# Attention and two MLPs on one core: seven block products in place of eight for x times w_in, and the MLP work put in order by a list scheduler

## The chip, the core and the metric

One core of a Trainium2 chip. The time is device microseconds of one execution. Engines: PE is TensorE (matrix products; PEld is its weight load), DVE is VectorE, ACT is ScalarE, POOL is GpSimd, SP issues the transfers. SBUF is the working memory, PSUM the eight banks (128 rows of 512 fp32) into which PE writes.

## The reference

Attention with rotary embedding over q, k, v (2 batches, 8 heads, 576 positions, 64 wide), then two MLPs one after the other on the 1152 tokens of width 512. The MLPs are what the change touches:

```python
def _moe_ref(x, w_in, w_out):           # x 1152x512, w_in 512x2048, w_out 2048x512
    h = x @ w_in
    sp = np.where(h > 20.0, h, np.log1p(np.exp(np.minimum(h, 20.0))))
    g = h * np.tanh(sp)
    return (g @ w_out).astype(np.float32)

def _moe2_ref(x, w_in, w_out):
    h = x @ w_in
    g = h * (1.0 / (1.0 + np.exp(-1.702 * h)))
    return (g @ w_out).astype(np.float32)
```

## The kernel before, in words

**Precision.** Each fp32 operand of an MLP product is kept as two tiles, a high part (the value rounded to fp32r by an ACT copy) and a low part (value minus high, by DVE). A product is the sum of three: high-high, high-low, low-high (`TERMS`, `X_LAST`). So every 128-deep step of a matrix product costs three matmuls.

**Weights.** w_in and w_out lie in HBM as float64. `Weights` (L474) fetches one piece of 128x512 numbers (512 KB) with one DMA from SP (L490), narrows it to fp32 bits with three DVE operations (L517, L520, L523), and splits it: ACT makes the high part (L504), DVE the low part (L505). `W.step` does the next of these five operations whenever the MLP code calls it, so the order of DVE and ACT is that of the calls.

**MLP one.** The 2048 columns of h are done in two halves of eight blocks of 128 (`FC` = 8). `phase_in` (L605) takes from `units_in` one unit after the other, a 128x384 piece of h transposed (block j of d_ff, third u of the tokens), 12 matmuls of 128x128 by 384 columns each (`mm_in`, L574). ACT applies the activation out of PSUM (L620) and copies the high part into g (L621), DVE subtracts the low part (L611). `phase_out1` (L627) then multiplies g by w_out (L641, 384 columns), keeps the first half's sums in `acc` (ACT, L1114) and adds the second half's (DVE, L1119), and splits the result into x2, the second MLP's input (L1120, L1121).

**MLP two** is the same with `phase_out2` (L652): here g is the stationary operand and w_out moves, 512 columns a matmul (L655). ACT keeps the first half (L1134), DVE adds the second (L1137), SP stores each tile of 128 tokens (L1148).

**Order.** Attention and the first ten steps of MLP one are ordered by `Plan`, a planner with costs and due times. After `plan.run()` every engine follows the order in which the MLP code is written. In PSUM, `mbank` hands out eight banks in turn.

Of the kernel before, what the change touches and what calls it, by code (L numbers as in the profile page):

```python
# [22 lines left out]
def kernel(  # L23
# [12 lines left out]
    nc = tc.nc  # L36
# [13 lines left out]
    FC = KF // 2  # L50
# [404 lines left out]
    def in_piece(w, j):  # L455
        return w[:, 128 * j:128 * j + 128].rearrange("(k p) c -> p k c", p=128)

    ORDER = ((0, 0), (1, 0), (2, 0), (0, 1), (1, 1), (2, 1), (3, 0), (3, 1))

    pieces = []  # L460
    for c in range(2):
        pieces += [in_piece(w_in1, FC * c + j) for j in range(FC)]
        for d, f in ORDER:
            f0 = 128 * FC * c + 512 * f
            pieces.append(w_out1[f0:f0 + 512, 128 * d:128 * d + 128].rearrange("(k p) c -> p k c", p=128))
    for c in range(2):
        pieces += [in_piece(w_in2, FC * c + j) for j in range(FC)]
        for f in range(FC):
            f0 = 128 * (FC * c + f)
            pieces.append(w_out2[f0:f0 + 128, :])  # L470

    RING = 11

    class Weights:  # L474
# [4 lines left out]
        def __init__(self):  # L479
            self.late = None  # L480
            self.loaded = self.narrowed = self.split = self.freed = 0
            self.raw, self.flat, self.parts = {}, {}, {}
            self.todo = deque()
            self.eng, self.ahead = DVE, 0

        def load_one(self):
            n = self.loaded
            t = self.raw[n] = wp.tile([128, 512], w_in1.dtype, tag="wraw", name="wraw", bufs=2)
            src = pieces[n]
            SP.dma_start(out=t.rearrange("p (k c) -> p k c", k=4) if len(src.shape) == 3 else t, in_=src)  # L490
            self.loaded += 1

        def load(self):
            while self.loaded < len(pieces) and self.loaded - self.narrowed < self.ahead:
                self.load_one()

        def start(self):
            if self.split < self.narrowed and self.split - self.freed < (RING if self.late else 3):
                n = self.split
                pool, bufs = (wp, 3) if n % RING < 3 else (self.late, RING - 3)  # L500
                r = self.flat.pop(n)
                t = self.parts[n] = pool.tile([128, 2, 512], F32R, tag="whl", name="whl", bufs=bufs)
                self.todo.extend([
                    lambda: ACT.activation(out=t[:, 0], in_=r, func=AF.Copy),  # L504
                    lambda: self.eng.tensor_tensor(out=t[:, 1], in0=r, in1=f32(t[:, 0]), op=ALU.subtract),  # L505
                ])
                self.split += 1
            elif self.narrowed < self.loaded and self.narrowed - self.split < 2:
                n = self.narrowed
                raw = self.raw.pop(n)  # L510
                if WIDE:
                    words = raw.bitcast(I32).rearrange("p (n w) -> p n w", w=2)
                    lo, hi = words[:, :, 0], words[:, :, 1]
                    t = wp.tile([128, 512], I32, tag="wf", name="wf", bufs=2)
                    self.flat[n] = f32(t)
                    self.todo.extend([
                        lambda: DVE.tensor_scalar(  # L517
                            t, hi, 3, 0x3FFFFFF8, op0=ALU.logical_shift_left, op1=ALU.bitwise_and
                        ),
                        lambda: DVE.scalar_tensor_tensor(  # L520
                            out=t, in0=hi, scalar=-0x40000000, in1=t, op0=ALU.bitwise_and, op1=ALU.bitwise_or
                        ),
                        lambda: DVE.scalar_tensor_tensor(  # L523
                            out=t, in0=lo, scalar=29, in1=t, op0=ALU.logical_shift_right, op1=ALU.bitwise_or
                        ),
                    ])
                else:
                    self.flat[n] = raw
                self.narrowed += 1

        def step(self, count=1):
            for _ in range(count):
                if not self.todo:
                    self.load()
                    self.start()
                if not self.todo:
                    return
                self.todo.popleft()()
            if not self.todo:
                self.load()  # L540

        def get(self, n):
            while self.split <= n or self.todo and n == self.split - 1:
                self.step()
            return self.parts[n]

        def free(self, n):

            del self.parts[n]
            while self.freed < self.split and self.freed not in self.parts:  # L550
                self.freed += 1
# [8 lines left out]
    def mbank(name):  # L560
        nbank[0] = nbank[0] % 8 + 1
        if nbank[0] <= 6:
            return pools["b"].tile([128, 512], F32, tag="b", name=name)
        return pvps if nbank[0] == 7 else bank(name)
# [14 lines left out]
    def units_in(n0, src, full=0):  # L579


        early = {}
        for j, u in sorted(((j, u) for j in range(2) for u in range(3)), key=lambda x: x[1] if full else 0):
            early[j, u] = mbank("h")
            mm_in(early[j, u], W.get(n0 + j), src, u, range(KD if u < full else KD - 1))
            yield None
        late = X_LAST[2:] if full else X_LAST
        for j, u in early:
            if u >= full > 0:
                mm_in(early[j, u], W.get(n0 + j), src, u, (KD - 1,), X_LAST[:2])  # L590
                yield None
        for j in range(FC):
            for u in range(3):
                if j < 2:
                    ps = early.pop((j, u))
                    if u >= full:
                        mm_in(ps, W.get(n0 + j), src, u, (KD - 1,), late)
                else:
                    ps = mbank("h")
                    mm_in(ps, W.get(n0 + j), src, u, range(KD))  # L600
                if u == 2:
                    W.free(n0 + j)
                yield j, u, ps[:, 0:UN]

    def phase_in(units, g, func):  # L605

        late = deque()

        def low():
            gl, t, gh = late.popleft()  # L610
            DVE.tensor_tensor(out=gl, in0=t, in1=f32(gh), op=ALU.subtract)  # L611

        for unit in units:
            W.step(2)
            if unit is None:
                continue
            j, u, ps = unit
            t = pools["tp"].tile([128, UN], F32, tag="t", name="t")
            gh, gl = (g[:, i, j, cols(u)] for i in range(2))
            ACT.activation(out=t, in_=ps, func=func)  # L620
            ACT.activation(out=gh, in_=t, func=AF.Copy)  # L621
            late.append((gl, t, gh))
            if len(late) > 1:
                low()
        low()

    def phase_out1(n0, g, evac):  # L627


        acc = {}  # L630
        steps = [(i, u) for i in range(len(ORDER)) for u in range(3)]
        steps.insert(11, steps.pop(8))
        for i, u in steps:
            d, half = ORDER[i]
            w = W.get(n0 + i)
            if half == 0:
                acc[d, u] = mbank("acc")
            ps = acc[d, u]
            for f in range(4):
                for wl, gl in TERMS:  # L640
                    PE.matmul(  # L641
                        out=ps[:, 0:UN], lhsT=w[:, wl, 128 * f:128 * f + 128], rhs=g[:, gl, 4 * half + f, cols(u)],
                        start=(half == 0 and f == 0 and (wl, gl) == TERMS[0]),
                        stop=(half == 1 and f == 3 and (wl, gl) == TERMS[2]),
                    )
            if u == 2:
                W.free(n0 + i)
            if half == 1:
                evac(d, u, ps[:, 0:UN])
            W.step(2)  # L650

    def phase_out2(n0, g, evac, by_tile):  # L652
        def mm(ps, t, f, w):
            for gl, wl in TERMS:
                PE.matmul(  # L655
                    out=ps, lhsT=g[:, gl, f, 128 * t:128 * t + 128], rhs=w[:, wl, :],
                    start=(f == 0 and (gl, wl) == TERMS[0]), stop=(f == FC - 1 and (gl, wl) == TERMS[2]),
                )
        ps = {t: mbank("acc") for t in range(5)}
# [536 lines left out]
```

## Time and profile before

| | |
|---|---|
| median of 3 runs | 557.73 us (557.49 to 558.0) |
| the profiled execution | 556.88 us; its trace spans 555.0 us |
| PE busy | 544.6 us, 98% of the span |
| DVE, ACT, POOL busy | 341.0, 257.5, 90.1 us |
| chain that ended last | 90% PE, 6% DVE, 2% DMA |
| granted TensorE clock | full (2.4 GHz) in every slice up to the last |

The MLPs begin at 147 us (first matmul of L574) and fill the rest. An engine's busy time is the union of its instructions. A matmul's record is longer than the time until the next one can start, since matmuls overlap in the array; what a stream of them costs is read from where the first and the last start, not from the mean of one.

### The profile page before, as it was taken

What the parts mean: (1) busy time and instruction counts of PE and PEld (TensorE: products, weight loads), DVE (VectorE), ACT (ScalarE), POOL (GpSimd) and SP (SyncE); (2) the same over time, 40 slices, a digit from 0 to 9 for tenths busy, and PEclk for the clock granted to TensorE, in tenths of its full rate; (3) what the DMA queues carried; (4) which work ended last, traced back from release to release, by engine and by line L of the source; (5) the groups of instructions that cost most, each with busy time, mean ns of one, the idle gap of its engine ahead of it and who ended that gap; (6) DMA issues with size and microseconds to landing.
All of it is one profiled execution on the core that took longest, in us unless ns stands there. A gap on an engine that the chain in (4) does not pass through costs nothing.

```text
span 555.0 us, 8983 instructions
## 1 busy us (share of the span) xinstructions
PE 544.6 (98%) x3517; PEld 489.9 (88%) x3517; DVE 341.0 (61%) x684; ACT 257.5 (46%) x544; POOL 90.1 (16%) x86
## 2 busy tenths in 40 slices
PE   8999999999999999999999999999999999999996
PEld 7876777777879999999999999999988899998885
DVE  6889889989629874356976458676520537820020
ACT  2887778887418741223865122275512126741000
POOL 3777868544100000000000000000000000000000
PEclk9999999999999999999999999999999999999999
DMA  7856596675505434233342322422310123200032
GB/s 201 186 121 162 112 211 151 133 118 137 145 1 152 124 107 150 64 123 118 119 139 85 114 77 76 141 83 81 96 57 1 61 88 121 73 1 0 1 113 57
DMA packets 82537, 56.90 MB, mean 103 GB/s; under 512 B 47224, under 2 KB 78272, under 8 KB 82496
## 3 DMA queue, kind: packets, MB, share of 16 engines
q1 hardware_dynamic: 81504, 56.12, 38.4%
q8 instruction: 27, 0.44, 0.3%
q10 hardware_dynamic: 992, 0.23, 0.2%
q14 instruction: 14, 0.11, 0.1%
HBM read 43.45 MB, written 2.40 MB: 83 GB/s over the span
## 4 chain that ended last, share of the span: by engine, by line
PE 90%; DVE 6%; DMA 2%; ACT 1%; issue 1%; SPq 1%; DVEq 0%; ACTq 0%
PE h L574 32%; PE acc L641 16%; PE acc L655 16%; PE st L261 5%; PE pvps L574 4%; PE pvps L421 4%; PE pvps L641 2%; PE st L334 2%; DVE spill L274 2%; PE pvps L655 2%; PE tps L232 2%; PE pvps L429 2%; DMA raw_v<-in_v_dram 1%; DVE pt L304 1%; DMA rest<-in_q_dram 1%
## 5 line engine op out<-in xcount | busy, mean ns | idle before, releaser
L574 PE MATMUL h<-x,whl 128*128 128x384 f32 x1008 | 179.5, 335 | 0.0
L574 PEld LDWEIGHTS h<-x,whl 128*128 128x128 f32 x1008 | 174.8, 188 | 2.9 <-issue 2.5
L505 DVE TENSOR_TENSOR whl<-wf,whl 128x512 fp32r<-128x512 f32 x62 | 42.9, 692 | 94.9 <-ACT whl L504 94.9
L655 PE MATMUL acc<-whl,g 128*128 128x512 f32 x384 | 88.9, 389 | 0.0
L641 PE MATMUL acc<-g,whl 128*128 128x384 f32 x504 | 88.6, 334 | 0.0
L641 PEld LDWEIGHTS acc<-g,whl 128*128 128x128 f32 x504 | 87.5, 188 | 0.0
L655 PEld LDWEIGHTS acc<-whl,g 128*128 128x128 f32 x384 | 72.0, 188 | 14.9
L611 DVE TENSOR_TENSOR g<-t,g 128x384 fp32r<-128x384 f32 x96 | 53.1, 554 | 27.1 <-ACT g L621 27.1
L504 ACT ACTIVATE whl<-wf 128x512 fp32r<-128x512 f32 x64 | 40.2, 628 | 62.1 <-DVE wf L523 42.8
L274 DVE CUSTOM_DVE_ANT_1 spill<-st,shift 128x576 f16<-128x576 f32 x72 | 54.4, 755 | 8.6 <-PE st L261 3.5
L620 ACT ACTIVATE t<-h 128x384 f32<-128x384 f32 x84 | 40.5, 482 | 35.8 <-PE h L574 35.8
L621 ACT ACTIVATE g<-t 128x384 fp32r<-128x384 f32 x96 | 50.6, 527 | 3.1
L289 ACT ACTIVATE e<-st,nm 128x576 f32<-128x576 f32 x64 | 47.1, 739 | 4.8 <-DVE nm L274 4.0
L261 PE MATMUL st<-qk 64*128 64x288 f32 (+1 forms) x432 | 44.3, 311 | 1.6 <-ACT e L289 1.5
L520 DVE SCALAR_TENSOR_TENSOR wf<-wraw,wf 128x512 int32<-128x512 int32 x64 | 44.2, 691 | 1.6
L261 PEld LDWEIGHTS st<-qk 64*128 64x128 f32 (+1 forms) x432 | 34.1, 185 | 12.6 <-ACT e L289 6.6
L523 DVE SCALAR_TENSOR_TENSOR wf<-wraw,wf 128x512 int32<-128x512 int32 x64 | 44.1, 689 | 1.4
L308 POOL TENSOR_TENSOR p<-e,p 128x576 f16<-128x576 f32 x28 | 38.0, 1371 | 28.1 <-DVE p L304 19.5
L1137 DVE TENSOR_TENSOR acc<-acc,acc 128x512 f32<-128x512 f32 x8 | 5.5, 687 | 37.1 <-PE acc L655 37.1
L574 PE MATMUL pvps<-x,whl 128*128 128x384 f32 x144 | 27.2, 334 | 0.0
L517 DVE TENSOR_SCALAR wf<-wraw 128x512 int32<-128x512 int32 x64 | 26.9, 420 | 0.0
L574 PEld LDWEIGHTS pvps<-x,whl 128*128 128x128 f32 x144 | 25.2, 188 | 0.0
(111 smaller groups left out, 506.0 us busy)
## 6 DMA issues: line engine op xcount, KB each, us to landing
wraw<-in_moe_w_in_dram SPq DMA_DIRECT2D x32, 512.0 KB, 3.7
wraw<-in_moe_w_out_dram SPq DMA_DIRECT2D x32, 512.0 KB, 3.5
rb<-scratch SPq DMA_DIRECT2D x16, 144.0 KB, 3.5
raw_v<-in_v_dram SPq DMA_DIRECT2D x4, 512.0 KB, 5.9
raw<-in_q_dram SPq DMA_DIRECT2D x3, 512.0 KB
raw<-in_k_dram SPq DMA_DIRECT2D x3, 512.0 KB, 4.7
out_dram<-acc SPq DMA_DIRECT2D x10, 128.0 KB, 2.3
out_dram<-acc SPq DMA_DIRECT2D x4, 256.0 KB
```

What stands on the lines that cost most here:

```text
L261: PE.matmul(out=st[:, g, 0:HALF], lhsT=t[r, ql, c0:c0 + 128], rhs=t[r, kl, KC + HALF * g:KC + HALF * g + HALF], start=(i == 0), stop=(i == 2),
L274: DVE.tensor_tensor_reduce(out=spill, in0=st[:, :, 0:HALF], in1=shift[:, 0:1].unsqueeze(2).to_broadcast([128, 2, HALF]), scale=-SCALE, sca ...
L289: ACT.activation(out=ebuf[p, n // 2][:, n % 2, :].rearrange("p (g s) -> p g s", g=2), in_=st[:, :, 0:HALF], func=AF.Exp, bias=nm, scale=SC ...
L505: lambda: self.eng.tensor_tensor(out=t[:, 1], in0=r, in1=f32(t[:, 0]), op=ALU.subtract),
L520: lambda: DVE.scalar_tensor_tensor(out=t, in0=hi, scalar=-0x40000000, in1=t, op0=ALU.bitwise_and, op1=ALU.bitwise_or),
L523: lambda: DVE.scalar_tensor_tensor(out=t, in0=lo, scalar=29, in1=t, op0=ALU.logical_shift_right, op1=ALU.bitwise_or),
L574: PE.matmul(out=ps[:, 0:UN], lhsT=w[:, wl, 128 * kk:128 * kk + 128], rhs=src[:, xl, kk, cols(u)], start=(kk == 0 and (wl, xl) == X_LAST[0] ...
L611: DVE.tensor_tensor(out=gl, in0=t, in1=f32(gh), op=ALU.subtract)
L620: ACT.activation(out=t, in_=ps, func=func)
L621: ACT.activation(out=gh, in_=t, func=AF.Copy)
L641: PE.matmul(out=ps[:, 0:UN], lhsT=w[:, wl, 128 * f:128 * f + 128], rhs=g[:, gl, 4 * half + f, cols(u)], start=(half == 0 and f == 0 and (w ...
L655: PE.matmul(out=ps, lhsT=g[:, gl, f, 128 * t:128 * t + 128], rhs=w[:, wl, :], start=(f == 0 and (gl, wl) == TERMS[0]), stop=(f == FC - 1 a ...
```

## The change

**Seven products.** `FC` is now 4: each MLP has four blocks of 512 columns of h (`NCH` = 4). The first block is done as before (12 units of 12 matmuls of 384 columns). In the other three the columns are taken in pairs of 128, and for each pair `flow_seven` computes x times w_in as a product of 2x2 blocks (depth in two halves of 256, columns in two of 128, tokens in two of 576) with seven block products in place of eight. Each product is two halves of 288 tokens with six matmuls each (L1509). The sums that it needs are new work:

- of the weights: four sums of 128x256 a pair, on POOL (`total`, L774), and the split of seven blocks in place of four (ACT L518, DVE L519),
- of x: per MLP eight differences of 128x576 on DVE (L1458), which are split too; in MLP one x is first put together from its parts (L1451),
- of the products: ACT copies out of PSUM (L1527) into the bank of the next product or into SBUF, products that accumulate onto what stands in a bank, and DVE additions of 128x288 from PSUM (L1542); then activation, high and low part as before.

**The weights** now come in pieces of 1 MB, narrowed 1024 numbers at a time (L507, L508, L511), through rings of two raw, two narrowed and two split tiles and three tiles `ws` of seven split blocks.

**g times w_out** has the same matmuls (L1333, L1326), now in four blocks: the first eight units are done in two halves of six matmuls, the rest whole. The first block's sums are kept by ACT (L1347), the others' added by DVE (L1350), so DVE adds three times where it added once.

**Order.** All MLP work after the first ten steps goes into `Flow`, which fixes PE's order (`STEPS` for a pair of columns: number of the product, a or b for the first or second pair, e and f for a unit of g times w_out of the block before or of this one), gives every operation a cost and a due time, and puts each engine's work in order by a list schedule.

```diff
-    FC = KF // 2
+    FC = 4
+    NCH = KF // FC
+    HT = TOK // 2
+    HH = HT // 2
...
+    PRODUCTS = {1: (0, "b11"), 2: (1, "b21"), 3: (6, "b22"), 4: (2, "t4"), 5: (3, "t1"), 6: (5, "t2"), 7: (4, "t3")}
+    STEPS = "1a e 2a 6a 5a 7a 1b 4a 3a 2b 6b 5b 7b f 4b 3b f f f"
...
+        LAG, TAIL, OVER = 0.13, 0.2, 0.08
...
+            for o in reversed(ops):
+                if o["eng"] != "PE":
+                    o["need"] = min(o["need"], t)
+                for d in o["deps"]:
+                    d["need"] = min(d["need"], o["need"] - d["cost"] - d["lead"] - self.LAG)
...
+                o = min((o for o in some if when(o) <= at + 0.03), key=lambda o: (o["need"], o["n"]))
+                start = max(at, when(o))
...
+                if o["shared"]:
+                    port["POOL" if e == "DVE" else "DVE"] = done
...
+            def total(i, a, b, op, deps, s=s, wf=wf, raw=raw):
+                return flow.add(
+                    "POOL", 0.75,
+                    lambda: POOL.tensor_tensor(out=kc(s["tile"][:, i]), in0=a(), in1=b(), op=op), deps, [s, wf, raw], True,
                 )
...
+            s1 = total(0, a21, a22, ALU.add, before)
+            s3 = total(1, a11, a21, ALU.subtract, before)
+            s2 = total(2, sums(0), a11, ALU.subtract, [s1])
+            s4 = total(3, a12, sums(2), ALU.subtract, [s2])
...
+    flow.ring("raw", 2, W.raw_tile)
+    flow.ring("wf", 2, W.flat_tile)
+    flow.ring("whl", 2, W.part_tile)
+    flow.ring("ws", 3, lambda: wl.tile([128, 2, 7, 256], F32R, tag="ws", name="ws", bufs=3))
+    flow.ring("s", 1, lambda: wl.tile([128, 4, 256], F32, tag="s", name="s", bufs=1))
+    flow.ring("g", 1, lambda: gp.tile([128, 2, FC, TOK], F32R, tag="g", name="g"))
...
+            for h in range(2):
+                def fn(ps=ps, h=h, i=i, name=name, key=key, n=n, m=m):
...
+                    for kk in range(2):
+                        for wl, xl in X_LAST:
+                            PE.matmul(
+                                out=ps[h]["tile"][:, 0:HH], lhsT=w[:, wl, i, 128 * kk:128 * kk + 128],
+                                rhs=ops[xl][:, kk, half(h)], start=(n in (1, 5) and kk == 0 and (wl, xl) == X_LAST[0]),
+                                stop=(kk == 1 and (wl, xl) == X_LAST[2]), skip_group_check=True,
+                            )
...
+                if n in (1, 6, 7):
...
+                    def keep(ps=ps, h=h, to=to, n=n):
+                        ACT.activation(out=to["tile"][:, 0:HH] if n == 1 else to["tile"][:, half(h)], in_=ps[h]["tile"][:, 0:HH], func=AF.Copy)
...
+                    halves_["wo"[n == 3], ab, h] = flow.add("DVE", dve(HH), lambda t=t, z=z, h=h: DVE.tensor_tensor(
+                        out=t["tile"][:, half(h)], in0=t["tile"][:, half(h)], in1=z[h]["tile"][:, 0:HH], op=ALU.add),
+                        deps, [t, z[h]])
```

**What moves: PE, second block of MLP one.** Up to the first matmuls of MLP one every engine's order is what it was. Then, where PE made unit after unit of h, twelve matmuls for one wait on ACT (before):

```order
L574 MATMUL h<-x,whl 128x384 [waits Activation_49]
L574 MATMUL h<-x,whl 128x384 x11
L574 MATMUL pvps<-x,whl 128x384 [waits Activation_49]
L574 MATMUL pvps<-x,whl 128x384 x11
L574 MATMUL h<-x,whl 128x384 [waits Activation_49]
L574 MATMUL h<-x,whl 128x384 [waits DVE_49]
L574 MATMUL h<-x,whl 128x384 x10
```

the first pair of columns of a block now reads as follows, from product 1 of the second pair on (products 4 and 3 of the first pair behind it; x, z and pvps are banks, xt the split differences of x, ws the seven split weight blocks):

```order
L1509 MATMUL x_2888<-x,ws 128x288 x6
L1509 MATMUL x_2896<-x,ws 128x288 x6
L1509 MATMUL x_2772<-xt,ws 128x288 [waits Activation_49]
L1509 MATMUL x_2772<-xt,ws 128x288 x5
L1509 MATMUL x_2781<-xt,ws 128x288 [waits Activation_49]
L1509 MATMUL x_2781<-xt,ws 128x288 x5
L1509 MATMUL pvps<-x,ws 128x288 [waits DVE_49]
L1509 MATMUL pvps<-x,ws 128x288 x5
L1509 MATMUL z<-x,ws 128x288 [waits DVE_49]
L1509 MATMUL z<-x,ws 128x288 x5
```

Groups of six 288-column matmuls stand where groups of twelve 384-column ones stood, and most groups begin with a wait on ACT or DVE for the result of a group a few places ahead.

**What moves: DVE, before the same products.** Before, DVE's rows in this place are the narrowing and splitting of one small piece and the low part of one unit of h in turn:

```order
L520 SCALAR_TENSOR_TENSOR wf_2601<-wraw_2519,wf_2601 128x512
L523 SCALAR_TENSOR_TENSOR wf_2601<-wraw_2519,wf_2601 128x512
L611 TENSOR_TENSOR g_2412<-t_2603,g_2412 128x384
L505 TENSOR_TENSOR whl_2640<-wf_2601,whl_2640 128x512
L611 TENSOR_TENSOR g_2412<-t_2624,g_2412 128x384
```

Now, in the rows that lead up to the addition t_2885 on which product 3 of the first pair waits (s_2680 and s_2826 are the tiles of POOL's weight sums):

```order
L519 TENSOR_TENSOR ws_2764<-wf_2678,ws_2764 128x512
L519 TENSOR_TENSOR xt_2411<-ws_2575,xt_2411 128x576
L519 TENSOR_TENSOR ws_2764<-wf_2678,ws_2764 128x256
L519 TENSOR_TENSOR ws_2646<-s_2680,ws_2646 128x512 x2
L507 TENSOR_SCALAR wf_2855<-wraw_2809 128x1024
L519 TENSOR_TENSOR ws_2764<-s_2826,ws_2764 128x512
L508 SCALAR_TENSOR_TENSOR wf_2855<-wraw_2809,wf_2855 128x1024
L519 TENSOR_TENSOR ws_2764<-s_2826,ws_2764 128x512
L511 SCALAR_TENSOR_TENSOR wf_2855<-wraw_2809,wf_2855 128x1024
L1542 TENSOR_TENSOR t_2885<-t_2885,pvps_77 128x288
```

The addition stands behind the splits of both pairs and behind the narrowing of the next piece of w_out. It is the 62nd DVE row after the last low part of x. The last addition before product 3 of the second pair in the next block, t_3502, is the 138th:

```order
L519 TENSOR_TENSOR g_3329<-t_3447,g_3329 128x576
L519 TENSOR_TENSOR ws_3485<-wf_3392,ws_3485 128x512
L519 TENSOR_TENSOR ws_3366<-wf_3311,ws_3366 128x256
L519 TENSOR_TENSOR ws_3485<-wf_3392,ws_3485 128x256
L1542 TENSOR_TENSOR t_3502<-t_3502,pvps_77 128x288
```

The tiles ws_3366 and ws_3485 in front of it belong to the block after that one.

**What moves: POOL.** Before, POOL had no work in the MLPs after its last split at 143 us. Now it has 48 sums of 128x256 (L774), four for each of the twelve pairs. They read the narrowed weights as soon as DVE has made them, and ACT and DVE split what they write. By the rows' numbers 20 of them stand ahead of t_3502, and four more beside it.

## Rows read from the trace of the kernel before

**Rows 1.** The page's busy times of the engines, and its chain that ended last.

```profile
PE 544.6 (98%) x3517; PEld 489.9 (88%) x3517; DVE 341.0 (61%) x684; ACT 257.5 (46%) x544; POOL 90.1 (16%) x86
...
PE 90%; DVE 6%; DMA 2%; ACT 1%; issue 1%; SPq 1%; DVEq 0%; ACTq 0%
```

**Rows 2.** Busy time by stage: MLP one, MLP two, the end.

```profile
core 0: us, PE busy (x) PEld busy (x) DVE busy (x) ACT busy (x) POOL busy (x), PEclk, DMA share, GB/s
164.00:352.00 188.00, 188.00 (x1086) 188.00 (x1086) 128.25 (x230) 81.37 (x159) 0.00 (x0) 1.00 0.37 113
352.00:550.00 198.00, 198.00 (x1011) 181.01 (x1009) 80.36 (x144) 66.50 (x129) 0.00 (x0) 1.00 0.20 62
550.00:555.00 5.00, 0.28 (x2) 0.00 (x0) 0.69 (x1) 0.00 (x0) 0.00 (x0) 0.93 0.23 52
```

**Rows 3.** The chain of waits: start us, us, step, count.

```profile
480.47 14.56 PE h L574 x84
402.33 27.92 PE acc L655 x123
```

**Rows 4.** Groups of PE instructions by shape: count, busy us, mean ns.

```profile
L574 PE MATMUL h<-x,whl 128*128 128x384 f32 x1008 | 179.5, 335 | 0.0
L574 PE MATMUL pvps<-x,whl 128*128 128x384 f32 x144 | 27.2, 334 | 0.0
```

**Rows 5.** PE in attention: timeline of full-depth matmuls of 288 columns.

```profile
17.76 0.82 PE L261 MATMUL st<-qk 128*128 128x288 f32 x5
...
18.29 0.29 PE L261 MATMUL st<-qk 128*128 128x288 f32 x1
```

**Rows 6.** Groups of DVE instructions by shape.

```profile
L611 DVE TENSOR_TENSOR g<-t,g 128x384 fp32r<-128x384 f32 x96 | 53.1, 554 | 27.1 <-ACT g L621 27.1
L505 DVE TENSOR_TENSOR whl<-wf,whl 128x512 fp32r<-128x512 f32 x62 | 42.9, 692 | 94.9 <-ACT whl L504 94.9
L517 DVE TENSOR_SCALAR wf<-wraw 128x512 int32<-128x512 int32 x64 | 26.9, 420 | 0.0
L520 DVE SCALAR_TENSOR_TENSOR wf<-wraw,wf 128x512 int32<-128x512 int32 x64 | 44.2, 691 | 1.6
```

**Rows 7.** Groups of POOL instructions by shape.

```profile
L308 POOL TENSOR_TENSOR p<-e,p 128x576 f16<-128x576 f32 x28 | 38.0, 1371 | 28.1 <-DVE p L304 19.5 <-issue 4.4 <-ACT p L302 2.6
L449 POOL TENSOR_TENSOR x<-xf,x 128x256 fp32r<-128x256 f32 x7 | 5.2, 740 | 8.3 <-ACT x L302 8.3
```

**Rows 8.** Timeline of DVE and POOL in attention: three stretches.

```profile
94.16 0.97 DVE L383 SCALAR_TENSOR_TENSOR rc<-sums,unit_of 128x9 f32<-128x9 f32 x1
...
93.82 1.28 POOL L194 TENSOR_TENSOR rtmp<-raw,rcos 128x512 f32<-128x512 f32 x1 [1.32 <-PE tps L232]
...
142.84 0.17 DVE L383 SCALAR_TENSOR_TENSOR rc<-sums,unit_of 128x9 f32<-128x9 f32 x1 [0.29 <-ACT e L289]
...
50.01 1.86 POOL L308 TENSOR_TENSOR p<-e,p 128x576 f16<-128x576 f32 x1 [3.65 <-DVE p L304]
```

**Rows 9.** Timeline of DVE, then PE, where attention's last x is split.

```profile
163.53 0.49 DVE L449 TENSOR_TENSOR x<-xf,x 128x320 fp32r<-128x320 f32 x1 [0.54 <-ACT x L302]
163.94 0.42 DVE L517 TENSOR_SCALAR wf<-wraw 128x512 int32<-128x512 int32 x1
...
163.55 1.65 PE L574 MATMUL h<-x,whl 128*128 128x384 f32 x8
165.05 0.33 PE L574 MATMUL pvps<-x,whl 128*128 128x384 f32 x1
```

**Rows 10.** Groups of ACT instructions by shape.

```profile
L620 ACT ACT_TABLE_LOAD x2 | 2.6, 1283 | 0.7 <-DVE x L449 0.7
L302 ACT ACTIVATE pr<-eps 128x320 f32<-128x320 f32 x4 | 1.7, 433 | 1.7 <-PE eps L364 1.7
```

**Rows 11.** The page's DMA issues: KB each, us from issue to landing.

```profile
wraw<-in_moe_w_out_dram SPq DMA_DIRECT2D x32, 512.0 KB, 3.5
```

**Rows 12.** Groups of weight loads (PEld) by shape.

```profile
L574 PEld LDWEIGHTS h<-x,whl 128*128 128x128 f32 x1008 | 174.8, 188 | 2.9 <-issue 2.5 <-DVE wf L517 0.2 <-ACT x L302 0.2
```

More of the change, by code (lines that the diff above doesn't have):

```diff
@@ L466, with rows @@
[L466 to L472, printed above, removed]
+    def rows(ap):
+        return ap.rearrange("(k p) c -> p k c", p=128)
+    jobs = []
+    for m, (w_in, w_out) in enumerate(((w_in1, w_out1), (w_in2, w_out2))):
+        for c in range(NCH):
+            ch = NCH * m + c
+            if c:
+                for i in range(2):
+                    j = FC * c + 2 * i
+                    jobs.append((("pair", ch, i), rows(w_in[:, 128 * j:128 * j + 256])))
+            else:
+                jobs += [(("one", ch, j), rows(w_in[:, 128 * j:128 * j + 128])) for j in range(FC)]
+            f = 128 * FC * c
+            for i in range(2):
+                src = w_out[f + 256 * i:f + 256 * i + 256, :] if m else w_out[f:f + 512, 256 * i:256 * i + 256]
+                jobs.append((("out", ch, i), rows(src)))
@@ L491, in load_one, with step @@
             self.loaded += 1
[L493 to L508, printed above, removed]
+        def step(self):
+            if not self.todo and self.narrowed - self.made < 1:
@@ L529, in start @@
                 self.narrowed += 1
[L531 to L538, printed above, removed]
-            if not self.todo:
[L540 to L551, printed above, removed]
+            if not self.todo:
+                n = self.made
+                if n % 2 == 0:
+                    self.tile = self.part_tile()
+                h = 512 * (n % 2)
+                t = self.parts[jobs[n][0]] = self.tile[:, :, h:h + 512]
+                self.todo.extend(self.split([t[:, i] for i in range(2)], self.flat.pop(n)[:, 0:512]))
+                self.made += 1
+            self.todo.popleft()()
     W = Weights()
@@ L577, in mm_in, with units_in @@
                 )
-    def units_in(n0, src, full=0):
+    EARLY = [(j, u) for u in range(3) for j in range(2)]
+    def units_in():
         early = {}
-        for j, u in sorted(((j, u) for j in range(2) for u in range(3)), key=lambda x: x[1] if full else 0):
+        for j, u in EARLY:
             early[j, u] = mbank("h")
-            mm_in(early[j, u], W.get(n0 + j), src, u, range(KD if u < full else KD - 1))
+            mm_in(early[j, u], W.parts["one", 0, j], x, u, range(KD if u == 0 else KD - 1))
@@ L586, in units_in @@
             yield None
[L587 to L590, printed above, removed]
+        for j, u in EARLY:
+            if u:
+                mm_in(early[j, u], W.parts["one", 0, j], x, u, (KD - 1,), X_LAST[:2])
                 yield None
[L592 to L597, printed above, removed]
-                else:
[L599 to L615, printed above, removed]
-                continue
[L617 to L657, printed above, removed]
-                )
-        ps = {t: mbank("acc") for t in range(5)}
-        for f in range(FC):
-            w = W.get(n0 + f)
-            for t in range(5):
-                mm(ps[t], t, f, w)
-                if f == FC - 1:
-                    evac(t, ps[t])
-                if t % 2:
-                    W.step(2)
-        for t in range(5, NT):
-            ps[t] = mbank("acc")
-        for i in range(FC * (NT - 5)):
-            t, f = (5 + i // FC, i % FC) if by_tile else (5 + i % (NT - 5), i // (NT - 5))
-            mm(ps[t], t, f, W.get(n0 + f))
-            if f == FC - 1:
-                evac(t, ps[t])
-            if t == NT - 1:
-                W.free(n0 + f)
-            if i % 4 == 3:
-                W.step(2)
+        yield early
@@ L1077 @@
         plan_pair(p)
[L1078 removed]
+    units = units_in()
     def swap():
[L1081 removed]
+        pools["b"] = stage("psum2", b=dict(bufs=1, space=PSUM))["b"]
     add("PE", 0.0, (END, "s"), swap, makes="swap",
@@ L1106 @@
     plan.run()
-    W.ahead = 2
-    pools.update(stage("sbuf", gp=dict(bufs=1), tp=dict(bufs=4), wl=dict(bufs=1)))
-    W.late = pools["wl"]
-    gp = pools["gp"]
+    early = next(units)
+    pools.update(stage("sbuf", gp=dict(bufs=1), tp=dict(bufs=1), wl=dict(bufs=1)))
+    gp, tp, wl = (pools[k] for k in ("gp", "tp", "wl"))
     acc = gp.tile([128, KD, TOK], F32, tag="acc", name="acc")
-    def keep1(d, u, ps):
-        ACT.activation(out=acc[:, d, cols(u)], in_=ps, func=AF.Copy)
-    def give1(d, u, ps):
-        a = acc[:, d, cols(u)]
-        xh, xl = (x2[:, i, d, cols(u)] for i in range(2))
-        DVE.tensor_tensor(out=a, in0=a, in1=ps, op=ALU.add)
-        ACT.activation(out=xh, in_=a, func=AF.Copy)
-        DVE.tensor_tensor(out=xl, in0=a, in1=f32(xh), op=ALU.subtract)
@@ L1151, with late @@
-    for c in range(2):
-        n0 = 4 * FC + 2 * FC * c
-        g = gp.tile([128, 2, FC, TOK], F32R, tag="g", name="g")
-        phase_in(units_in(n0, x2), g, AF.Gelu_apprx_sigmoid)
-        phase_out2(n0 + FC, g, (keep2, give2)[c], c == 1)
+    xt = gp.tile([128, 2, 3, 2, HT], F32R, tag="xt", name="xt")
+    big = dict(acc=acc, x=x)
+    def late(name):
+        if name not in big:
+            if name == "x2":
+                big[name] = xp.tile([128, 2, KD, TOK], F32R, tag="x", name="x2")
+            else:
+                big[name] = gp.tile([128, NT, 512], F32, tag="acc", name="acc2")
+        return big[name]
@@ new lines, in in_unit, with fn @@
+    def in_unit(ch, j, u, b, ks, terms, slots, made, ready_x, which):
+        key = ("one", ch, j)
+        def fn():
+            if not terms:
+                return
+            src = late(which)
+            for kk in ks:
+                for wl, xl in terms:
+                    PE.matmul(
+                        out=b["tile"][:, 0:UN], lhsT=W.parts[key][:, wl, 128 * kk:128 * kk + 128],
+                        rhs=src[:, xl, kk, cols(u)],
+                        start=(kk == 0 and (wl, xl) == X_LAST[0]), stop=(kk == KD - 1 and (wl, xl) == X_LAST[2]),
+                    )
+        need = [made.get(key)] + [ready_x[kk, u] for kk in ks if (kk, u) in ready_x]
+        return pe(len(ks) * len(terms), UN, fn, need, [b, slots[key]])
@@ new lines, in store, with put @@
+    def store(t, dep):
+        def put():
+            r = 0
+            while r < 128:
+                b, j = divmod(128 * t + r, S)
+                k0, k1, c = next(x for x in ((0, 128, 0), (128, 256, 1), (256, 384, 2), (384, MAIN, 3), (MAIN, S, None))
+                                 if x[0] <= j < x[1])
+                n = min(128 - r, k1 - j)
+                if c is None:
+                    rows_ = out[b * S + MAIN:b * S + S, :]
+                else:
+                    rows_ = out[b * S:b * S + MAIN, :].rearrange("(p t) c -> t p c", t=4)[c]
+                SP.dma_start(out=rows_[j - k0:j - k0 + n, :], in_=late("acc2")[r:r + n, t, :])
+                r += n
+        flow.add("SP", 0.4, put, [dep])
@@ L1158 @@
+    flow_all()
+    flow.run()
 _INS = ['q', 'k', 'v', 'moe_w_in', 'moe_w_out', 'moe2_w_in', 'moe2_w_out']
```

494 lines of the change are left out of this document (437 added, 57 removed).

## Prediction

> **What bounds the kernel now.** I read the page first, then the stages, the chain, the groups. PE is busy for 98% of the span and is 90% of the chain that ended last [rows 1]. By stage, PE is busy for all 188 us of MLP one and all 198 us of MLP two, at full clock, while DVE has 128 and 80 us of work there, ACT 81 and 67, POOL none [rows 2]. So from 164 us on nothing but PE's own stream sets the time; a matmul saved is time saved, as long as the others keep up. The chain gives the price of a matmul in that stream: 84 of 384 columns take 14.56 us, 173.3 ns each, and 123 of 512 columns 27.92 us, 227 ns each [rows 3]. Those are the columns at 2.4 GHz (160 and 213 ns) and 13 to 14 ns more.
>
> **What PE saves.** x times w_in is 1152 matmuls of 384 columns [rows 4], 576 in each MLP. The first quarter stays. The other three quarters are 864 matmuls: 864 x 173.3 ns = 149.7 us. In their place the order has 1008 of 288 columns (12 pairs of column blocks, 7 products, 2 halves, 6 matmuls). Such matmuls over the full depth, each with its weight load, are in attention: five in a row, the first at 17.76 and the last at 18.29 us [rows 5], so 0.53 / 4 = 0.1325 us; I take 133 ns (120 ns of columns and 13). 1008 x 133 ns = 134.1 us. **PE saves 15.7 us.** The products of g and w_out are the same matmuls in another order: nothing. The start is the same up to the first matmuls of MLP one, and the end too: the last tile's 24 matmuls become 12 with the same addition and store behind them; the 5.0 us from 550 to the end [rows 2] stay.
>
> **What the others get.** ACT copies of 288 columns: one of 320 takes 433 ns [rows 10]. PE's waits on such a copy have at least one half product and one half unit of g times w_out between them (0.8 + 1.04 us) against some 0.3 us for the matmul's own length beyond its slot, 0.43 for the copy and a tenth for two handovers. I count them at nothing; ACT's larger splits are the cover's limit (1.1 us by twice the row of 512). Transfers: 512 KB land in 3.5 us [rows 11], so 1 MB in at most 7; the ring asks for a piece over 5 us before it is needed in the first block and far more later. I count that at nothing too, half a microsecond at most.
>
> **DVE is the term that decides.** A DVE operation on SBUF takes 554 ns for 384 and 692 for 512 elements [rows 6]: 140 ns and 1.08 ns an element. So I take 0.416 us for 256, 0.450 for 288, 0.761 for 576, 1.244 for 1024 and 1.382 for 1152, and for the first narrowing step, 420 ns for 512 [rows 6], 0.70 for 1024. Back to back each starts 80 ns before the one ahead ends (163.53 + 0.49 against 163.94) [rows 9]. A later block of MLP one then needs 4 x (0.70 + 2 x 1.244) narrowing, 2 x 1.244 and 2 x (3 x 0.692 + 0.416) splitting, 8 x 0.761 low parts, 8 x 0.450 and 12 x 0.554 additions: 36.6 us, less 50 x 0.08, is 32.6. PE needs 168 x 0.133 + 144 x 0.173 = 47.3. In the long run DVE keeps up.
>
> At the start it does not have the long run. The first block adds the sums and splits of x. From DVE's free start at 163.94 us [rows 9] to the addition t_2885 stand 62 operations: 2 and 10 second and third narrowing steps of 512 and 1024, 1 and 5 first steps, 4 of 1152, 2 of 1024, 16 of 576, 7 of 512, 12 of 384, one of 288, 2 of 256: 50.7 us, less 61 x 0.08, is 45.8, so 209.8 us. PE stands at its second matmul with x's low part at 164.53 (third before 165.05) [rows 9], and reaches the wait after 219 x 0.1733 + 84 x 0.133 = 49.1 us, at 213.6. To t_3502 in the next block it is 138 operations: 108.5 us, less 11.0, is 97.5: 261.4 us; PE is there after 369 x 0.1733 + 324 x 0.133 = 107.0 us, at 271.5. DVE alone has 4 and 10 us to spare.
>
> **POOL takes them.** Its sums of 128x256 cost about what its subtraction of that size did, 740 ns [rows 7]. The trace shows that the two engines shut each other out: a DVE operation on 9 elements takes 0.17 us alone and 0.97 us when a POOL operation of 1.28 us is under way, ending when that ends; a POOL operation that mostly takes 1.28 took 1.86 [rows 8]. Ahead of t_2885 stand 8 sums, 5.9 us; ahead of or beside t_3502 20 to 24, 14.8 to 17.8 us. With all of it on DVE's path DVE is 2.0 us late for the first and 4.7 to 7.7 us for the second. Less: 25 of the 138 additions read PSUM and may run beside POOL (12.5 of 97.5 us, so some 2 us). More: DVE's first low part of g waits for ACT's table load of 1.28 us [rows 10], about 1 us. The bounds are 0 (no shutting out) and 8; I take 5.5, by the trace's own contention. Past that block DVE works ahead. In MLP two the differences of x come from `acc` without putting x together, and DVE has over 8 us to spare at the first pair; in the later blocks the additions behind product 7 of a second pair stand close (PE's two groups of work and DVE's are equal there within the handovers): 0.5 us in each of three blocks, 1.5. The first product of g and w_out in MLP one waits for DVE's split of w_out with next to nothing to spare: 0.5. Together 7.5 us of new waits.
>
> **Sum.** Of the profiled execution's 556.88 us (span 555.0): -15.7 + 7.5 = -8.2, 548.7 us. The median of the runs shown is 0.85 above that execution, so **549.5 us**, as 557.73 - 8.2.
>
> **Rivals.**
> 1. *DVE is in time* (0.17). POOL slips into the gaps, or beside operations with one SBUF input. PE's saving stays, less at most 2 us: 542 to 544.5. For: DVE alone has 4 and 10 us. Against: rows 8.
> 2. *Slower: the shutting out costs more than POOL's own time* (0.12). Each sum waits for DVE's running operation, and DVE for the sum, and the handover is lost on both sides. Place: DVE's path to t_3502, with 24 sums. If a sum takes 1.37 us of that path, as POOL's 576-element operations do with their waits [rows 7], DVE needs 97.5 + 32.9 = 130.4 us against PE's 107.0, 23.4 late: 557.73 - 15.7 + 23.4 + 2 = 567. It decides from (107.0 + 15.7 - 97.5) / 24 = 1.05 us a sum. Against: the plain 128x256 row at 740 ns.
> 3. *Waits in every pair* (0.14). Each of the twelve pairs has five waits on ACT copies and four on DVE additions that did not exist; with 0.4 to 1 us lost in each pair on top of my sum it is 553 to 558.5. For: two engines' orders fixed by estimated costs. Against: the covers above.
> 4. *The weight load sets the pace of the shorter matmuls* (0.01). A load's record is 188 ns [rows 12]; if a matmul of 288 columns could not start before its own load had run behind the one ahead, 1008 would cost 189.5 us, 39.8 more than the 864 do now, and the time would be 605 us. Against: five such matmuls with five loads at 133 ns each [rows 5], and 173 ns between the 384-column ones [rows 3], both shorter than the load's record, so loads run beside matmuls here. The Trainium skill ("TensorE: Matmul & The Clock Gate", Part 3, The mechanism) has the rule behind this rival: a load overlaps with matmuls in flight only when the row groups differ, which full-depth ones never do. This trace does not bear it out.
>
> That the change does not do what it says is excluded by the order: 1008 matmuls.
>
> **How the numbers follow.** My forecast, DVE late by 3 to 9 us in all, has 0.56: 545 to 553. The range that holds it eight times in ten runs from rival 1's 542 to 557.5, into rival 3, and leaves out rival 2 and a part of 3. A difference of over 0.2% (1.1 us) is about what a measurement of this kernel can tell from none. Faster by that: forecast, rival 1 and two thirds of 3: 0.82. Within it: the rest of 3, 0.05. Slower: rivals 2 and 4, 0.13.
>
> **What would show it.** Right: the 1008 matmuls start 133 ns apart within a group; PE has its first idle time in the MLPs between 200 and 275 us, ended by DVE (t, ws) in the second and third block of MLP one, 3 to 8 us in all; DVE is busy there nearly throughout; POOL's sums come at 0.74 us or more. Wrong: idle time of PE spread over all pairs and ended by ACT; POOL and DVE overlapping without loss; PE idle before a weight split with a transfer as its releaser.

## The result, and the profile after

The changed kernel takes 548.18 us (median of 4 runs, 547.04 to 549.29) against 557.61 us for the kernel before beside it; ratio 0.983, 95% interval 0.981 to 0.986. The forecast was 549.5 us in 542 to 557.5. The number held; the place in which it put the new waits did not.

The profiled execution took 549.29 us with a span of 547.3, and its first matmul of MLP one came 1.7 us later than before, ahead of anything that the change touches. Page, busy time of the engines and granted clock by slice (answers to [rows 1]):

```profile
PE 531.4 (97%) x3661; PEld 476.2 (87%) x3661; DVE 416.5 (76%) x710; ACT 289.5 (53%) x616; POOL 151.6 (28%) x134
...
PEclk9999999999999997999999999999999999999999
```

DVE has 75.5 us more, POOL 61.5, ACT 32; PE has 144 matmuls more and 13 us less. One slice of the clock, the sixteenth, has a 7. Busy time by stage, first as in [rows 2], then the stretch around that slice:

```profile
core 0: us, PE busy (x) PEld busy (x) DVE busy (x) ACT busy (x) POOL busy (x), PEclk, DMA share, GB/s
164.00:352.00 188.00, 184.22 (x1168) 183.51 (x1167) 149.16 (x219) 92.61 (x188) 27.65 (x24) 0.98 0.27 85
352.00:540.00 188.00, 188.00 (x1074) 171.40 (x1073) 135.21 (x182) 87.60 (x173) 33.81 (x24) 1.00 0.26 87
...
164.00:200.00 36.00, 35.95 (x209) 35.49 (x208) 34.64 (x45) 21.86 (x44) 8.65 (x4) 1.00 0.37 118
200.00:203.50 3.50, 3.50 (x25) 3.50 (x24) 3.50 (x5) 1.45 (x3) 0.13 (x1) 1.00 0.00 0
203.50:207.60 4.10, 0.36 (x4) 0.13 (x2) 4.06 (x8) 2.34 (x6) 0.00 (x0) 0.79 0.75 250
207.60:213.00 5.40, 5.40 (x19) 5.40 (x20) 2.26 (x5) 2.07 (x5) 2.85 (x4) 0.53 0.01 5
213.00:230.00 17.00, 17.00 (x130) 17.00 (x129) 14.72 (x20) 12.47 (x27) 0.37 (x1) 1.00 0.34 103
```

PE is still full in both MLPs but for one hole (idle time in its stream) of some 4 us, and behind it the clock is granted at 0.53, the lower of its two levels (1.2 of 2.4 GHz). The list of PE's waits from 164 us to 540 us has that one entry (who waits, for whom, us in total, times, longest):

```profile
PE pvps L1333 <- ACT acc L1347: 3.7, 1, 3.7
```

PE's timeline there (start, us; in brackets idle time before and what ended it):

```profile
200.02 2.24 PE L1333 MATMUL pvps<-g,whl 128*128 128x384 f32 x12
202.10 1.74 PE L1509 MATMUL x<-x,ws 128*128 128x288 f32 x12
207.58 4.21 PE L1333 MATMUL pvps<-g,whl 128*128 128x384 f32 x12 [3.74 <-ACT acc L1347]
211.59 1.59 PE L1509 MATMUL y<-x,ws 128*128 128x288 f32 x7
```

The unit of g times w_out at 200.02 takes 2.24 us; the next one, behind the hole, 4.21. By the starts of the matmuls the hole costs 3.9 us (from the last start before it to the first behind it, less one period) and the 17 slow periods behind it 2.4: 6.3 us. Twelve matmuls of 288 columns at 202.10 take 1.74 us, so eleven periods of 132 ns; over all 1002 undisturbed ones the period is 132.6 ns, where 133 was forecast. PE's saving is therefore 864 x 173.35 - 1008 x 132.6 = 16.1 us. The time behind the start of the last matmul is 5.4 us, where it was 5.1 before; over the runs below it is 4.9 to 5.4. With these, -16.1 + 6.3 + 1.7 + 0.4 = -7.7 is the difference of the spans, 555.0 to 547.3.

Why the bank came late stands in ACT's timeline of the same stretch:

```profile
201.75 0.48 ACT L1347 ACTIVATE acc<-x 128x384 f32<-128x384 f32 x1
205.26 0.63 ACT L518 ACTIVATE ws<-wf 128x512 fp32r<-128x512 f32 x1 [3.03 <-DVE xt L519]
205.80 0.47 ACT L1347 ACTIVATE acc<-x 128x384 f32<-128x384 f32 x1
206.17 0.67 ACT L518 ACTIVATE xt<-ws 128x576 fp32r<-128x576 f32 x1
206.74 0.40 ACT L518 ACTIVATE ws<-wf 128x256 fp32r<-128x256 f32 x1
207.05 0.48 ACT L1347 ACTIVATE acc<-pvps 128x384 f32<-128x384 f32 x1
```

The unit at 200.02 is done at 202.26, and its copy, `acc<-pvps`, could run then. But ACT stands still for 3.03 us in front of the split `ws<-wf`: the second pair's weights go into the `ws` buffer that the differences of x still hold, and the last reader of those is DVE's split that ends at 205.23. The copy stands four places behind, in order, and PE wants its bank for the next unit.

DVE and POOL ahead of that, from their timelines:

```profile
191.20 4.84 POOL L774 TENSOR_TENSOR s<-wf 128x256 f32<-128x256 f32 x1 [44.84 <-DVE wf L511]
196.12 1.59 POOL L774 TENSOR_TENSOR s<-s,wf 128x256 f32<-128x256 f32 x1
...
192.75 2.08 DVE L1458 TENSOR_TENSOR ws<-ws 128x576 f32<-128x576 f32 x3
...
195.47 1.64 DVE L508 SCALAR_TENSOR_TENSOR wf<-wraw,wf 128x1024 int32<-128x1024 int32 x1
197.04 2.49 DVE L519 TENSOR_TENSOR xt<-ws,xt 128x576 fp32r<-128x576 f32 x2
199.46 1.29 DVE L1458 TENSOR_TENSOR ws<-ws 128x576 f32<-128x576 f32 x1
```

Three DVE operations of 576 elements take 2.08 us undisturbed; then two take 2.49 and one 1.29, and 1024 elements take 1.64 in place of 1.22: the four sums of the first pair cost DVE 2.0 us, 0.5 us each.

The rest is in the planner. `Flow` works out start times while the kernel is built; beside the trace's they are (us):

```
                                       Flow     trace    trace - Flow
PE   unit of w_in's third piece, L1425  3.76    166.73   162.97
PE   unit of g, w_out before the hole  36.98    200.02   163.04
DVE  last sum of x, L1451              20.23    186.60   166.37
DVE  last difference of x, L1458       36.86    205.15   168.29
ACT  split ws<-wf                      37.07    205.26   168.19
ACT  copy acc<-pvps                    39.38    207.05   167.67
```

In `Flow`'s world the copy can start at 39.38 and the split at 37.07, so the split goes first. On the chip PE is 3.4 us ahead of that world (162.97 against 166.37). The cause is a line of the code: a user of a buffer slot may not start before the slot's first user, and the first user that `Flow` knows of in the early `whl` slot is the split of another piece into its second half. So its PE waits 3.07 us in the unit of w_in's third piece for the split of the fourth, which it does not read; the real PE does not wait there. Between the two DVE rows the offset grows by another 1.9 us, about what POOL's four sums cost DVE.

### The profile page after: what moved, and what is told of

The parts are those of the page before. It is cut to its first block, busy times and chain, and to the rows that moved or that the text cites. A ratio compares the mean times of both kernels' runs of the same rounds, so it can differ in the third digit from the quotient of the medians.

```text
span 547.3 us, 9356 instructions
## 1 busy us (share of the span) xinstructions
PE 531.4 (97%) x3661; PEld 476.2 (87%) x3661; DVE 416.5 (76%) x710; ACT 289.5 (53%) x616; POOL 151.6 (28%) x134
## 4 chain that ended last, share of the span: by engine, by line
PE 78%; DVE 13%; ACT 4%; DMA 3%; issue 1%; SPq 1%; DVEq 0%; ACTq 0%
PE x L1509 14%; PE x L1326 8%; PE x L1333 6%; PE y L1333 5%; PE y L1326 4%; PE st L264 4%; PE y L1509 4%; PE z L1509 4%; PE pvps L1326 3%; PE pvps L1509 3%; PE pvps L424 3%; PE pvps L1333 3%; PE x L1425 2%; DVE spill L277 2%; DMA raw_v<-in_v_dram 2%; PE z L1326 2%
## 5 line engine op out<-in xcount | busy, mean ns | idle before, releaser
L774 POOL TENSOR_TENSOR s<-wf 128x256 f32<-128x256 f32 x24 | 37.0, 1556 | 270.0 <-DVE wf L511 225.2
L519 DVE TENSOR_TENSOR g<-t,g 128x576 fp32r<-128x576 f32 (+1 forms) x72 | 51.7, 736 | 15.9 <-ACT g L518 15.6
L1509 PE MATMUL x<-xt,ws 128*128 128x288 f32 x432 | 63.1, 295 | 0.0
L277 DVE CUSTOM_DVE_ANT_1 spill<-st,shift 128x576 f16<-128x576 f32 x72 | 54.3, 754 | 8.5 <-PE st L264 3.5
L1509 PEld LDWEIGHTS x<-xt,ws 128*128 128x128 f32 x432 | 59.5, 188 | 0.2
L1333 PE MATMUL x<-g,whl 128*128 128x384 f32 x264 | 49.0, 334 | 0.0
L1326 PE MATMUL x<-whl,g 128*128 128x512 f32 x192 | 46.1, 389 | 0.0
L1333 PEld LDWEIGHTS x<-g,whl 128*128 128x128 f32 x264 | 46.0, 188 | 0.0
L518 ACT ACTIVATE g<-t 128x576 fp32r<-128x576 f32 (+1 forms) x72 | 44.6, 631 | 0.8
L508 DVE SCALAR_TENSOR_TENSOR wf<-wraw,wf 128x1024 int32<-128x1024 int32 (+1 forms) x36 | 42.3, 1176 | 0.3
L1326 PEld LDWEIGHTS x<-whl,g 128*128 128x128 f32 x192 | 36.0, 188 | 7.5
L511 DVE SCALAR_TENSOR_TENSOR wf<-wraw,wf 128x1024 int32<-128x1024 int32 (+1 forms) x36 | 41.1, 1141 | 0.3
L518 ACT ACTIVATE whl<-wf 128x1024 fp32r<-128x1024 f32 (+1 forms) x24 | 22.0, 920 | 27.3 <-PE z L1333 11.4
L1333 PE MATMUL y<-g,whl 128*128 128x384 f32 x168 | 31.4, 334 | 0.0
L1527 ACT ACTIVATE y<-x 128x288 f32<-128x288 f32 x24 | 9.4, 397 | 41.4 <-PE x L1509 41.3
L1527 ACT ACTIVATE t<-x 128x288 f32<-128x288 f32 x48 | 19.6, 412 | 20.3 <-PE x L1509 20.0
L1350 DVE TENSOR_TENSOR acc<-acc,y 128x384 f32<-128x384 f32 (+1 forms) x19 | 11.4, 601 | 24.1 <-PE y L1326 15.0
L1333 PEld LDWEIGHTS y<-g,whl 128*128 128x128 f32 x168 | 29.1, 188 | 0.0
```

Source lines behind the costliest of these rows:

```text
L277: DVE.tensor_tensor_reduce(out=spill, in0=st[:, :, 0:HALF], in1=shift[:, 0:1].unsqueeze(2).to_broadcast([128, 2, HALF]), scale=-SCALE, sca ...
L508: lambda: DVE.scalar_tensor_tensor(out=t, in0=hi, scalar=-0x40000000, in1=t, op0=ALU.bitwise_and, op1=ALU.bitwise_or),
L511: lambda: DVE.scalar_tensor_tensor(out=t, in0=lo, scalar=29, in1=t, op0=ALU.logical_shift_right, op1=ALU.bitwise_or),
L518: lambda: ACT.activation(out=out[0], in_=in_, func=AF.Copy),
L519: lambda: self.eng.tensor_tensor(out=out[1], in0=in_, in1=f32(out[0]), op=ALU.subtract),
L774: lambda: POOL.tensor_tensor(out=kc(s["tile"][:, i]), in0=a(), in1=b(), op=op), deps, [s, wf, raw], True,
```

## The experiments

Three theories: **A**, the order (the copy behind the split, from the planner's error, with POOL's sums making DVE later still); **B**, DVE has too much to do up to there in any order; **C**, POOL's shutting out alone. All ratios are to the kernel before on the same chip.

**The planner mended.** An empty entry becomes the first user of those slots:

```diff
+        for slot in first:
+            flow.add("PE", 0.0, lambda: None, (), [slot])
         bank0 = {}
```

> The planner alone is mended: an empty PE entry is the first user of the two early whl buffers, so that its PE no longer waits 3.07 us (in its own reckoning) for a split that the third unit of the first block does not read. The changed kernel took 548.18 us, with one wait of PE in the MLPs, 3.74 us at 203.84 for a bank that ACT had still to copy out, and 12 + 8 slow matmuls behind it (about 2.4 us). Theory A (the planner takes PE to be 3 us later than it is, so ACT gets the split that waits for the ws buffer ahead of the copy; POOL's four sums, 0.5 us of DVE each, do the rest): the wait at the copy goes; the planner then expects 1.6 us of wait at the first product that needs POOL's sums, and with the sums at 1.2 to 1.6 us instead of 0.75 this is 2 to 4 us, ended by DVE or POOL: 544 to 548. Theory B (DVE simply has too much work up to there, no order helps): a wait of 3.5 us or more stays, 547.5 to 550. Theory C (the lock alone, the planner's error is harmless): the wait at the copy stays as it is, 548.2.

542.91 us, ratio 0.974 (0.972 to 0.976): 5.3 us less than the change as it was. The copy now stands ahead of the split (200.87 and 201.69 us), the clock stays, and two short waits are left, for the split of the sums:

```profile
PE x L1511 <- ACT ws L518: 0.6, 1, 0.6
PE x L1511 <- DVE ws L519: 0.3, 1, 0.3
```

A is right in kind and said too much: 2 to 4 us of wait were expected and 0.9 came, and the time is 1.1 us below A's bounds. POOL's first sum there is worth a look:

```profile
189.12 14.74 POOL L774 TENSOR_TENSOR s<-wf 128x256 f32<-128x256 f32 x1 [44.16 <-ACT acc L1349]
```

An operation of 0.74 us stands for 14.74 us, while DVE runs 20 operations one behind the other, each starting before the one ahead has ended; it ends 0.6 us after DVE's first gap begins, at 203.26 us. So this run moved two things: with POOL kept out until then, DVE ended its split of xt 2.2 us earlier after the first matmul of MLP one than in the changed kernel (54.3 us against 56.5). It does not tell the order from POOL by itself; the run with the copy first, below, does.

**The sums on DVE**, the planner's error left in: `"POOL", 0.75` becomes `"DVE", dve(256)` and `POOL.tensor_tensor` becomes `DVE.tensor_tensor`.

> The 48 sums of weights go from POOL to DVE, the planner's error stays. Theory A: DVE pays 4 x 0.34 = 1.4 us in place of about 2.0 us of shutting out ahead of the late copy, so the wait there falls from 3.7 to about 3.2 us and the slow matmuls stay: 547 to 548. Theory B (too much DVE work): DVE has 16 us more to do in all, waits in later blocks appear: 549 to 556. Theory C (the lock is the cause): the wait falls under 2 us: 543 to 546.

542.90 us, 0.974 (0.972 to 0.976): outside what A expected, and nearest to C. Yet the trace gives A's mechanism: with other costs the planner's order came out with the copy ahead of the split,

```profile
200.23 0.49 ACT L1347 ACTIVATE acc<-pvps 128x384 f32<-128x384 f32 x1 [0.32 <-PE pvps L1333]
203.55 0.63 ACT L518 ACTIVATE ws<-wf 128x512 fp32r<-128x512 f32 x1 [2.83 <-DVE xt L519]
```

so ACT's stall of 2.83 us is still there and now holds back only the copies of y, for which PE waits 0.7 us (and 0.5 later on, for a copy to t). The edit moved two things at once; my expectation had counted one, so this run decides nothing between A and C.

**Both.**

> Both edits: the planner mended and the sums on DVE. Theory A: DVE's order is planned against PE's true time and no sum waits for POOL: no wait of PE over 0.3 us in the MLPs, no slow matmuls: 548.18 - 3.7 - 2.4 = 542.1 us (541.5 to 543). Theory B (too much work on DVE at the start): 3 us or more of wait, 546 to 550. Theory C (the lock alone): as in the run with the sums on DVE alone.

541.19 us (540.91 to 541.55), 0.971 (0.969 to 0.974), 0.3 below A's bounds. PE has no wait at all from 164 to 537 us. DVE has 48 operations more (710 before the edit) and is hardly busier for it (418.3 against 416.5 us): its other operations of both MLPs are 12 us shorter in all than in the changed kernel, where POOL worked beside them. Its page:

```profile
PE 529.4 (98%) x3661; PEld 474.7 (88%) x3661; DVE 418.3 (78%) x758; ACT 290.2 (54%) x616; POOL 90.2 (17%) x86
```

556.99 - 541.19 = 15.8 us: PE's saving, within what the runs differ by. This version beats both kernels.

**The sums left out**, the planner's error left in: the splits read parts of `flat()` in place of `s`.

> The 48 sums of weights are left out: the splits read parts of the narrowed weights as they are (this part of the computation is left out). POOL has no work in the MLPs, DVE's own list is the same and the planner's error stays. Theory A: of the wait at the late copy, 3.74 us, the 2.0 us that four DVE operations lost to POOL go, 1.5 to 2 us stay, and the slow matmuls with it or not: 544 to 546.5. Theory B: the same 2 us or less go. Theory C (the lock is the whole cause): no wait over 0.3 us, 542. If the lock costs nothing: 548.2.

545.36 us, 0.978 (0.976 to 0.980). Without any work on POOL the wait at the same copy is still there:

```profile
PE pvps L1328 <- ACT acc L1342: 2.6, 1, 2.6
```

and so is ACT's stall in front of a split:

```profile
197.35 0.69 ACT L518 ACTIVATE xt<-ws 128x576 fp32r<-128x576 f32 x1 [0.79 <-DVE ws L1453]
202.43 1.15 ACT L518 ACTIVATE ws<-wf 128x512 fp32r<-128x512 f32 x2 [3.25 <-DVE xt L519]
203.48 0.67 ACT L518 ACTIVATE xt<-ws 128x576 fp32r<-128x576 f32 x1
204.05 0.47 ACT L1342 ACTIVATE acc<-pvps 128x384 f32<-128x384 f32 x1
```

C falls: by this run POOL was some 1.2 of the 3.74 us and the order the rest; ACT's list in front of the copy is not quite the same here, so the 1.2 is an estimate.

**The copy first.** Nothing taken away, planner's error and POOL's sums left in; in `flow_weights`, for the second pair of MLP one's second block alone:

```diff
+            if key == ("pair", 1, 1):
+                W.t4["deps"].append(W.copy)
+                before = before + [W.copy]
```

(`W.copy` is the last copy out of an out bank that was planned by then, `W.t4` ACT's split of the last difference.)

> As the change, with the planner's error and POOL's sums left as they are; only, the ACT splits that open the second pair's weights, and the last one of the differences of x, are told to wait for the copy of the out bank pvps, so that the copy stands ahead of them in ACT's queue. No work is taken away. Theory A (PE waits because the copy stands behind splits that wait for DVE): the wait of 3.74 us at that copy goes and with it the slow matmuls; some of it may come back a little later at the copies of y or at the products that need the sums: 0 to 1.5 us, so 542.2 to 544.5. Rival (DVE's lateness itself is what PE feels, the copy was only its first place): 2.5 us or more of wait stay in the following products, 545.5 to 548.5.

542.72 us, 0.975 (0.973 to 0.977). ACT copies pvps ahead of the split that waits for DVE:

```profile
200.59 0.50 ACT L1350 ACTIVATE acc<-pvps 128x384 f32<-128x384 f32 x1
...
203.37 0.64 ACT L518 ACTIVATE ws<-wf 128x512 fp32r<-128x512 f32 x1 [0.61 <-DVE xt L519]
```

Of the 3.74 us one wait of 0.9 is left, ten microseconds later:

```profile
PE x L1513 <- ACT t L1531: 0.9, 1, 0.9
```

That wait has the same form on a smaller scale: the copy for which PE waits, at 213.32 us, stands behind a split of w_out that itself waited 2.19 us for DVE.

This settles it against B. The work is the same on the same engines; the list schedule set six of ACT's operations, the copy among them, ahead of the split `ws<-wf`. PE's order is the same throughout, and so is DVE's up to the split of xt for which ACT stood still: DVE ends that one 56.5 us after the first matmul of MLP one in both runs. DVE is exactly as late as before, and 5.5 us come back (5.2 against the kernel before on each chip). Behind that place the orders of DVE and of POOL's sums differ a little.

**Half of the change.** Seven products in MLP two alone:

```diff
-            if c:
+            if c and m:
```

in the list of pieces and, likewise, where a block chooses between plain units and `flow_seven`.

> Seven products in MLP two alone; MLP one's later blocks keep the eight plain ones (576 matmuls of 384 columns in all), under the same list scheduler, with no sums of x or of weights there. Half of the matmul saving, 15.7 / 2 = 7.85 us, is left. Theory A (what the whole change loses, it loses at one late copy in MLP one's second block; the scheduler by itself neither gains nor loses): no wait of PE over 0.3 us, no slow matmuls, 557.0 - 7.85 = 549.2 us (548.5 to 550): half of the change is worth nearly all that the whole gave. Rival (the scheduler itself gains or loses some microseconds, or MLP two loses time that the trace does not show): under 547.5 or over 551.

549.38 us, 0.986 (0.984 to 0.988), no wait. Half of the change is worth 7.95 us, against 9.4 for the whole as it was; MLP one under the scheduler and with eight products neither gains nor loses anything beyond the 1.1 us of the interval.

**All but one block.** MLP one's second block plain, the others with seven products (`c > 1 or c and m`).

> Seven products everywhere but in MLP one's second block, which keeps the eight plain ones: five sixths of the saving, 13.1 us. The planner's error and POOL's sums stay. Theory A (the loss comes only where the differences of x and the first sums of weights meet the first block's splits): DVE gets a block's time for the differences, no wait over 0.5 us: 557.0 - 13.1 = 543.9 us (543.2 to 545). Rival (the wait belongs to the change wherever it begins): 3 us of wait and the slow matmuls in the third block: 547 to 550.

543.91 us, 0.976 (0.974 to 0.978), no wait; in this run t1 took the place of a quarter of x before the plain block had read it. With that difference put in place after the block:

> Seven products everywhere but in MLP one's second block, as in the run before, but the difference t1 takes the place of a quarter of x only after the second block has read it (in the run before it took it earlier, so the second block multiplied t1 in place of that quarter: that part of the computation was changed). Theory A: the same, no wait over 0.5 us, 13.1 us less than before: 543.9 (543 to 545). Rival (the later difference is late now): a wait of 1 us or more at the first products of the third block that read t1, 545 to 547.

544.10 us, 0.977 (0.975 to 0.978), no wait. The two agree with five sixths of the saving (13.1 us). With a block's time more, the same sums and the same planner's error cost nothing.

## Why the prediction was right, and where it was not

- *PE saves 15.7 us*: right. 132.6 ns a matmul against 133; the version without waits gains 15.8. *Rival 4* falls with it: 1008 matmuls start closer together than the 188 ns that the record of each one's weight load lasts. (Its 605 us also kept the 7.5 us of waits, for which a slower PE would have left more cover.)
- *7.5 us of new waits*: 6.3 were lost, so the sum held, by luck and not by its steps. The term of 5.5 us, DVE late at t_2885 and t_3502, is nil: with the copy put right and POOL's sums left in, PE reaches both without waiting for DVE, which has 2.0 and 2.2 us to spare. It was mis-sized because I put each sum's own 0.74 us on DVE's path, 15 to 18 us in all. Against the durations of the version with no work on POOL, DVE's operations of MLP one are 4.0 us longer in the changed kernel, 0.17 us a sum on average (half of the 4.0 us at the first four sums): POOL mostly waits for DVE, not the reverse. The terms of 0.5 us at the first split of w_out and of 1.5 us in MLP two are nil too.
- *ACT copies counted at nothing*: this is the step that failed. I weighed the length of the copies against the work between a unit and the next user of its bank, and named ACT's larger splits as the cover's limit, 1.1 us. What I left out is that a split can itself wait, for a buffer that DVE holds, and that ACT works in order: 3.03 us of standing still in front of a copy that was ready. Half of my own sign against the forecast, idle time of PE ended by ACT, came true, though in one place and not over all pairs. DVE's lateness does reach PE, but through ACT's queue and not by an addition that PE waits for.
- *The clock*: not in the sum. The lower level behind the hole took 2.4 of the 6.3 us. Behind 2.56 us of idle time (the run without sums) the next unit took 3.91 us in place of 2.24; behind the waits of 0.5 to 0.9 us in the other runs the granted clock stayed at 1.00.
- *Rival 1*, DVE in time, 542 to 544.5: this is what the change would have been with the copy in its place (542.7).
- *Rival 2* fell with the same measure: a sum takes 0.17 us of DVE's path on average and 0.5 at the most costly place, far from the 1.05 at which it decides. *Rival 3*: one pair of twelve waits, not all.

## What to carry to other kernels

When a change adds work to an engine that works in order, look at what can stall at its head and what ready work then stands behind it; the length of the operations does not show that. A scheduler in the kernel is only as good as its picture: lay its start times beside the trace, engine by engine, and a constant offset between two engines points at a wait that it made up. A short hole in a full TensorE can cost more than its length: here 3.74 us of idle time were followed by 2.4 us lost at the lower clock.

## What the runs showed that I had not expected

POOL does not take its turn between two DVE operations that follow without a gap: the 0.74 us sum stood for 4.84 us in the changed kernel and for 14.74 us with the planner mended. Both ended after DVE's first gap; that in the changed kernel was 35 ns, at 195.44 us. The Trainium skill ("SBUF — State Buffer", SBUF: two separate sides) says that of a DVE operation with two SBUF inputs and a POOL operation that reads SBUF, whichever starts first gets the shared port pair for the whole instruction while the other fully blocks. The trace is in line with that, and shows that back-to-back DVE instructions keep POOL out across their boundaries. Once in, the sums and DVE's operations alternated, and each of those DVE operations was 0.4 to 0.5 us longer.
